# PV of three late head pairs with P as the weight in a decode kernel of two attention and MLP layers

## The chip, the cores and the metric

The kernel runs on one core of one Trainium2 chip. The metric is the time of one execution on the device, in microseconds; lower is better. Three executions of the kernel before took 303.86, 305.12 and 305.42 us, with a median of 305.12 us.

## The reference

Four sequences decode one token each. A layer is an attention block and a gated MLP, and two such layers run one after the other with the same weights and the same K and V caches:

```python
x = x + _A_ref(_layernorm(x), A_k_cache, A_v_cache, A_wq, A_wo)
x = x + _B_ref(_layernorm(x), B_w_gate, B_w_up, B_w_down)
```

In `_A_ref`, q = x @ wq gives 32 heads of 128; four query heads share one of 8 K/V heads (grouped queries); scores over 4096 keys are scaled, a softmax gives P, the output of a head is P @ V, and all heads go through `wo`. Everything is bf16 at the border; K and V of one sequence and head are 4096 x 128, 1 MB each. `_B_ref` is sigmoid(x @ w_gate) * (x @ w_up) @ w_down with 1792 hidden features.

## The kernel before, in words

The work on the caches is cut into **units**: one layer, one sequence, one K/V head. Two neighbouring heads make a **pair** g; there are 32 pairs, in the order of the list `ORDER`. K and V of a unit are one slot each of SBUF, 32 keys to a partition. There are 12 slots, and four more once wq is done with. `RET` says which units of the first layer stay in SBUF for the second; the last three pairs before the end, 28, 29 and 30, belong to layer 1, sequence 3, and have their K (and one V) kept, so that only V of 56, 58, 59, 60 and 61 and K and V of the last pair's units 62 and 63 are loaded for them. All loads are issued by SyncE in the order of `LOADS`, by `pump` (L522), which issues as many as there are free slots; it is called wherever a slot comes free.

The main loop (L1821) has one iteration k for each pair. It scores the pair sg = k and does PV of the pair vg = k - 1. Instructions of an engine run in program order. Each pair goes through these steps, with the lines at which they are recorded:

- `k_turn` (L1149, record L1164): VectorE transposes K in place, whole or in two halves.
- `scores` (L1166, record L1180): q as the weight, K as the moving operand, 256 columns a matmul, over four strips of 32 PSUM partitions. 16 matmuls a unit.
- `smax` (L1213), `spread_max` (L1236, record L1240), `softmax` (L1250; the exponential is L1265, on ScalarE): the row maximum on VectorE, spread over the rows by TensorE, then exp. The sums are split on GpSimd (L1279), and `sums` (L1283, record L1288) and `inverse` bring 1/sum to all partitions.
- `ptrans` (L1305, record L1310): TensorE transposes P into PSUM (`PT`). P is then copied to `pT` in 16 pieces of 32 partitions, `SHARE[g]` groups of four on VectorE (L1338), the others on ScalarE (L1344). With `SHARE[g]` 6 it is a single ScalarE copy (L1325), the exponential writes P in another order of keys, and V comes in four pieces of 2 KB a partition (`by_quarters`, L503), since the order of keys over partitions differs. Pair 29 is such a pair, and so is pair 31, whose V is loaded in single pieces of 256 KB by `v_parts` (L510).
- `pv` (L1349), once for each unit: V as the weight (128 x 128), P as the moving operand, 4 columns repeated up to `PV_WIDE[g]` columns. 32 matmuls a unit, recorded at L1414, or at L1364 where V comes in quarters. The result stands with a head's 128 features on the partitions.
- `normalise` (L1496, record L1505): VectorE multiplies by 1/sum into `oT`.
- `wo_mm` (L1515): a pair's part of wo. With `WO_ROW[g]` 0, 32 matmuls with wo as the weight (L1566). With 1 or 2, oT is the weight and wo moves over four strips (L1536), ScalarE copies the rows out (L1545) and two fp32 matmuls with the selector `sel_f` turn them into columns (L1549); with 2 this turn comes later, at the next `do_steps`. `wo_add` (L1587) adds to x.

`PV_WIDE[g] < 2` chooses another way in `pv`: P as the weight, V moving, two strips for each unit. No pair uses it in the kernel before; `o_turn` (L1474) belongs to it.

Where a step stands within the iteration is written out in tables. For the iterations that matter here: in iterations 29 and 30 PV of pairs 28 and 29 comes after the exponential of the iteration's own pair, both units one behind the other; in iteration 31 the first unit of pair 30 comes before the spread of the maximum of pair 31, the second after its exponential is issued. Wo of pair 28 is in iteration 30, of pair 29 in iteration 31 (its turn delayed), of pair 30 after the loop's last scores, in iteration 32. Then follow PV of pair 31 (`pv_last`, L1431, record L1441), its wo (L1775), the last MLP (L920, L2018) and the output.

Of the kernel before, what the change touches and what calls it, by code (L numbers as in the profile page):

```python
# [5 lines left out]
dt = mybir.dt  # L6
# [98 lines left out]
)  # L105
# [41 lines left out]
)  # L147
# [6 lines left out]
}  # L154


# [154 lines left out]
def bass_interleave_layers__gqa_block_cached__glu_gated_glu__decode_kernel(  # L311
# [73 lines left out]
    mask_f = sbt([P, 4, 2, 4, REP], dt.bfloat16, "mask_f")  # L385
    sel_f = sbt([P, 2, 2], dt.float32, "sel")
    SEL = 2 * REP * any(w < 2 for w in PV_WIDE)
    o_sel = sbt([P, 2, SEL], dt.float32, "o_sel") if SEL else None
    strip_b = sbt([P, 16], dt.bfloat16, "strip_b")
# [6 lines left out]
    xc_sb = sbt([P, KD, Bn], dt.float32, "xc")  # L396
    norm = sbt([P, KD + 10, Bn], dt.float32, "norm")
    sq_sb, newt = norm[:, 0:KD + 1, :], norm[:, KD + 1:, :]
    lnsum, blk_f, vpe, nt_a, nt_b, nt_c, nt_y, rs = [newt[:, i, :] for i in range(8)]
    y0i = newt[:, 8, :].bitcast(dt.int32)  # L400
    xc_bf = sbt([P, KD, Bn], dt.bfloat16, "xc_bf")
# [258 lines left out]
    def head_masks():  # L660
# [15 lines left out]
        for u in range(2):  # L676
# [29 lines left out]
        )  # L706
        id4 = ident_bf.rearrange("p (u e w) -> p u e w", u=2, e=2)
        dve(
            lambda e: e.tensor_tensor(sel_f[:, :, :], id4[:, :, 0, 0:2], id4[:, :, 1, 0:2], ALU.add),
            reads=IDENT,  # L710
            writes=["sel"],
        )
        if SEL:
            dve(
                lambda e: e.tensor_tensor(o_sel[:, :, :], id4[:, :, 0, 0:SEL], id4[:, :, 1, 0:SEL], ALU.add),
                reads=IDENT,
                writes=["o_sel"],
            )
        if SEL or any(WO_ROW):
# [585 lines left out]
    def ptrans(g):  # L1305
# [15 lines left out]
        if SHARE[g] > 5:  # L1321
            to = pT.rearrange("p x n j h -> p (x n j h)")
            keys = [f"pT_{x}{a}" for x in range(XJ) for a in ("", "_0", "_1", "_2")]
            if SHARE[g] == 6:
                act(lambda e: e.activation(to, PT[:, 0:2 * P], ACTF.Copy), reads=["PT"], writes=keys)  # L1325
            else:
                dve(lambda e: e.tensor_copy(to, PT[:, 0:2 * P]), reads=["PT"], writes=keys)
            return
        src = PT[:, 0:256].rearrange("p (n a h) -> p n a h", n=16, h=REP)
        for x in range(XJ):  # L1330
            for a in range(4):
                dst = pT[32 * a:32 * a + 32, x].rearrange("p n j h -> p j n h")
                frm = src[32 * x:32 * x + 32, :, a, :].rearrange("p (j n) h -> p j n h", j=2)
                key = f"pT_{x}"
                wr = [key if a == 3 else f"{key}_{a}"]
                if x in (1, 3)[:SHARE[g]]:
                    dve(
                        (lambda dst, frm: lambda e: e.tensor_copy(dst, frm))(dst, frm),  # L1338
                        reads=["PT"],
                        writes=wr,  # L1340
                    )
                else:
                    act(
                        (lambda dst, frm: lambda e: e.activation(dst, frm, ACTF.Copy))(dst, frm),  # L1344
                        reads=["PT"],
                        writes=wr,
                    )

    def pv(i):  # L1349
# [6 lines left out]
        if by_quarters(i):  # L1356
# [20 lines left out]
            if l == 1 or not kept("v", i):  # L1377
                free.append(where.pop(("v", b, u)))
            return
        if PV_WIDE[g] < 2:  # L1380
            many = 2 - PV_WIDE[g]
            for x in range(XJ):
                fns = []
                for m in range(4 // many):
                    at = 2 * ul + m % 2
                    fns.append(
                        (lambda x, m, at: lambda e: e.matmul(
                            O_ps[p][32 * at:32 * at + 8 * many, 0:2 * P * many],
                            lhsT=pT[:, x, 4 * ul + many * m:4 * ul + many * (m + 1), :, :].rearrange("p c j h -> p (c j h)"),
                            rhs=vv[:, x * JG + 2 * many * m:x * JG + 2 * many * (m + 1), :],  # L1390
                            start=(x == 0 and m < 2),
                            stop=(x == XJ - 1 and m >= 4 // many - 2),
                        ))(x, m, at)
                    )
                key = f"pT_{x}"
                rd = [f"s{s}", key] + [f"{key}_{a}" for a in range(3)]
                if ul == 0 and x == 0:
                    S.group("pe", fns, reads=rd, writes=[f"O{p}"])
                else:
                    S.last_write[f"O{p}"] = S.group("pe", fns, reads=rd)  # L1400
            done = l == 1 or not kept("v", i)
            if ul == 0:
                stage.clear()
            elif done and stage:
                free.append(stage.pop())
            if done:
                stage.append(where.pop(("v", b, u)))
            return
# [64 lines left out]

    def o_turn(g):  # L1474
        p = g % 2
        many = 2 - PV_WIDE[g]
        s = stage.pop()
        o_raw = slot[s].bitcast(dt.float32)[:, 0:2 * P * many]
        act(lambda e: e.activation(o_raw, O_ps[p][:, 0:2 * P * many], ACTF.Copy), reads=[f"O{p}"], writes=slot_keys(s))
        fns = []  # L1480
        for n in range(2 * many):
# [9 lines left out]
            )  # L1491
        S.group("pe", fns, reads=slot_keys(s) + ["o_sel"], writes=[f"O{p}"])
        free.append(s)
        pump()

    def normalise(g):  # L1496
        if PV_WIDE[g] < 2:
            o_turn(g)
        l, b, u = seq[2 * g]
# [321 lines left out]
    for k, (sg, vg) in enumerate(plan):  # L1821
# [34 lines left out]

        def pv_second():
            pv(2 * vg + 1)
            pump()

        def divide():
            normalise(vg)
            normed[seq[2 * vg]] = k
# [29 lines left out]
        if pv_first and both:  # L1893
            pv(2 * vg)
            pump()
            if pv_both:
                pv_second()
# [17 lines left out]
        if both and not pv_first and not pv_late:  # L1915
            pv(2 * vg)
            pump()
        wo_at(2)
        do_steps(k, 5)
        second_turn(1)  # L1920
        if pv_late:
            pv(2 * vg)
            pump()
        if sg == NP - 1 and LAST & 3 == 0:
# [39 lines left out]
        if sg is not None and sg != NP - 1:  # L1964
            ptrans(sg)
        wo_at(3)
        do_steps(k, 7)
        second_turn(2)
        if vg is not None and sg is not None and vg in ends:
            close(vg, k)  # L1970
        if k == NP - 3:
            wo_sums()
        if sg is not None and EARLY[sg]:
            sums(sg)
            inverse(sg)
            for ul in range(2):
                pv(2 * sg + ul)
                pump()
            normalise(sg)
            normed[seq[2 * sg]] = k  # L1980
            if sg in ends:
# [150 lines left out]
```

## Time and profile before

| What | Value |
|---|---|
| Median of three timed executions | 305.12 us |
| Span of the profiled execution, first to last instruction | 306.1 us |
| TensorE matmul busy | 224.3 us, 73% of the span, 4993 instructions |
| VectorE busy | 205.7 us, 67% |
| ScalarE busy | 131.2 us, 43% |
| GpSimd busy | 26.0 us, 9% |
| Moved from HBM | 116.66 MB, 381 GB/s over the span |
| Mean granted TensorE clock | 0.883 |
| Chain that ended last | DMA 45%, PE 30%, DVE 12%, SPq 5%, ACT 4%, issue 3% |

The span of 306.1 us is the profiled execution's own time; the timed executions are others. The chain is the work that ended last, followed back from the last instruction, each step to what released it. "Issue" in it is time in which an engine waited for nothing that the profile shows. PE is TensorE, PEld its weight loads, DVE VectorE, ACT ScalarE, POOL GpSimd, SP SyncE. An instruction is named by the line of the kernel that made it, its output and its inputs, with the shape as partitions x elements. All shares are means over the whole span; the stretch that the change touches is the last 30 us of it.

### The profile page before, as it was taken

How to read it: one execution, taken by the hardware profiler on the slowest of the kernel's cores; microseconds unless marked ns; L12 is line 12 of the kernel's file. 1: busy time of each engine (PE TensorE's matmuls, PEld its weight loads, DVE VectorE, ACT ScalarE, POOL GpSimd, SP SyncE). 2: the span in 40 equal slices, each digit the busy share in tenths (PEclk: the TensorE clock that was granted, in tenths of full speed). 3: DMA queues.
4: the chain of work that ended last, by engine and by line, in shares of the span. 5: the costliest groups of instructions: out<-in, count | busy, mean ns of one | idle time of the engine just before them, and what ended most of it. 6: DMA issues, size and time to landing. Idle time of an engine off the chain costs nothing.

```text
span 306.1 us, 11460 instructions
## 1 busy us (share of the span) xinstructions
PE 224.3 (73%) x4993; PEld 157.6 (51%) x4993; DVE 205.7 (67%) x600; ACT 131.2 (43%) x521; POOL 26.0 (9%) x107
## 2 busy tenths in 40 slices
PE   0384386864687888688886777888868688987886
PEld 0331043543464466566554554665546456556676
DVE  4755677885766368875854997566788668357743
ACT  1031243552205246564451874627772443646310
POOL 0000000000000010000001110001000000012200
PEclk9999999999579897979999857589788979599977
DMA  7999999999999979999999999999999999999900
GB/s 283 420 397 415 422 414 416 418 418 421 418 416 403 388 295 418 423 415 416 388 394 378 415 422 421 419 418 422 420 416 418 413 412 415 400 345 411 377 18 3
DMA packets 20094, 117.40 MB, mean 384 GB/s; under 512 B 1992, under 2 KB 1996, under 8 KB 7500
## 3 DMA queue, kind: packets, MB, share of 16 engines
q1 hardware_dynamic: 20044, 116.67, 93.9%
q8 instruction: 39, 0.64, 0.8%
q14 instruction: 11, 0.09, 0.1%
HBM read 116.66 MB, written 0.00 MB: 381 GB/s over the span
## 4 chain that ended last, share of the span: by engine, by line
DMA 45%; PE 30%; DVE 12%; SPq 5%; ACT 4%; issue 3%; POOL 0%; POOLq 0%; DVEq 0%; ACTq 0%
DMA slot<-in_A_v_cache_dram 22%; DMA slot<-in_A_k_cache_dram 12%; PE O_ps L1414 9%; DMA wd<-in_B_w_down_dram 6%; DVE slot L1164 6%; DMA wo<-in_A_wo_dram 5%; PE S_ps L1180 5%; ACT pT L1344 2%; SPq L550 2%; SPq L528 2%; PE M_ps L636 2%; PE O_ps L1566 2%; PE M_ps L1034 1%; PE M_ps L1087 1%; DVE wo L651 1%
## 5 line engine op out<-in xcount | busy, mean ns | idle before, releaser
L1164 DVE STREAM_TRANSPOSE slot<-slot 128x1024 f32<-128x1024 f32 (+1 forms) x61 | 100.9, 1663 | 7.0 <-DMA slot<-in_A_k_cache_dram 6.9
L1344 ACT ACTIVATE pT<-PT 32x64 bf16<-32x64 f32 x392 | 84.3, 215 | 31.9 <-PE PT L1310 26.9
L1414 PE MATMUL O_ps<-pT,slot 128*128 128x32 bf16 (+2 forms) x1888 | 65.8, 190 | 16.2 <-DMA slot<-in_A_v_cache_dram 9.6
L1414 PEld LDWEIGHTS O_ps<-pT,slot 128*128 128x128 bf16 x1888 | 59.6, 101 | 23.3 <-DMA slot<-in_A_v_cache_dram 10.6
L1180 PE MATMUL S_ps<-slot,qz 128*32 128x256 bf16 x1008 | 48.9, 329 | 12.5 <-DVE slot L1164 7.2
L1265 ACT ACTIVATE pe<-S_ps,small 128x256 bf16<-128x256 f32 x32 | 15.2, 474 | 63.3 <-DVE small L1253 63.2
L1180 PEld LDWEIGHTS S_ps<-slot,qz 128*32 128x32 bf16 x1008 | 25.3, 107 | 24.8 <-DVE slot L1164 9.2
L1279 POOL TENSOR_TENSOR small<-small 128x1 f32<-128x1 f32 x64 | 12.4, 193 | 217.6 <-ACT pe L1265 215.1
L646 ACT ACTIVATE wo<-M_ps 128x512 bf16<-128x512 f32 x14 | 8.3, 595 | 35.0 <-PE M_ps L636 35.0
L1338 DVE CAST pT<-PT 32x64 bf16<-32x64 f32 x88 | 19.4, 221 | 5.6 <-PE PT L1310 4.1
L1566 PE MATMUL O_ps<-oT,wo 128*128 128x32 bf16 x576 | 19.7, 188 | 1.1 <-issue 0.5
L636 PE MATMUL M_ps<-wo,row 64*128 64x512 bf16 x56 | 13.3, 565 | 9.1 <-DVE wo L651 5.5
L1566 PEld LDWEIGHTS O_ps<-oT,wo 128*128 128x128 bf16 x576 | 18.2, 101 | 2.1 <-DVE oT L1505 1.1
L1217 DVE TENSOR_REDUCE small<-S_ps 128x1 f32<-128x256 f32 x32 | 13.2, 413 | 8.0 <-PE S_ps L1180 7.8
L903 POOL TENSOR_TENSOR qz<-qc,norm 128x128 bf16<-128x128 bf16 x32 | 12.6, 399 | 45.5 <-ACT qc L889 45.5
L1240 PE MATMUL MS<-row_max,mask_f 128*128 128x16 bf16 x64 | 6.6, 176 | 13.1 <-DVE row_max L1223 12.6
L651 DVE CAST wo<-M_ps 128x512 bf16<-128x512 f32 x14 | 9.5, 680 | 9.6 <-PE M_ps L636 9.5
L1505 DVE TENSOR_TENSOR oT<-O_ps,rden 128x8 bf16<-128x8 f32 x31 | 4.9, 159 | 14.4 <-PE O_ps L1414 9.8
L1240 PEld LDWEIGHTS MS<-row_max,mask_f 128*128 128x128 bf16 x64 | 4.3, 107 | 19.2 <-DVE row_max L1223 17.7
L1199 PE MATMUL MS<-ident_bf 128*128 128x256 bf16 x69 | 12.2, 316 | 0.4
L1310 PE MATMUL PT<-ident_bf,pe 128*128 128x128 bf16 x64 | 10.0, 245 | 2.9 <-ACT pe L1265 2.6
L1253 DVE CUSTOM_DVE_ANT_0 row_max<-MS,small 128x16 bf16<-128x16 f32 x32 | 7.0, 217 | 7.3 <-PE MS L1240 7.1
(143 smaller groups left out, 231.1 us busy)
## 6 DMA issues: line engine op xcount, KB each, us to landing
slot<-in_A_v_cache_dram SPq DMA_DIRECT2D x49, 1024.0 KB, 12.5
slot<-in_A_k_cache_dram SPq DMA_DIRECT2D x43, 1024.0 KB, 11.3
wq<-in_A_wq_dram SPq DMA_DIRECT2D x4, 1024.0 KB, 7.8
wo<-in_A_wo_dram SPq DMA_DIRECT2D x8, 512.0 KB, 15.8
wq<-in_A_v_cache_dram SPq DMA_DIRECT2D x3, 1024.0 KB, 12.3
slot<-in_A_v_cache_dram SPq DMA_DIRECT2D x8, 256.0 KB, 13.6
wg<-in_B_w_gate_dram SPq DMA_DIRECT2D x2, 896.0 KB, 18.9
wu<-in_B_w_up_dram SPq DMA_DIRECT2D x2, 896.0 KB, 16.2
```

What stands on the lines that cost most here:

```text
L636: (lambda h, i, rows: lambda e: e.matmul(ps[h][:, :], lhsT=spread_w[i][rows, :], rhs=wo_sb[rows, c + i, :], start=(i == 0), stop=(i == 1), ...
L651: lambda e: e.tensor_copy(wo_sb[:, c + 1, :], ps[1][:, :]),
L903: lambda e: e.tensor_tensor(qz_sb[z][:, :, 0:4 * REP].rearrange("p i (a r) -> p i a r", r=REP), qc_sb[:, b, u:u + 2, :, :].rearrange("p u ...
L1164: dve(lambda e: e.transpose(kf, kf), writes=[f"s{st}"])
L1180: (lambda t, b2, e_, w0, s: lambda e: e.matmul(S_ps[p][32 * s:32 * s + 8 * REP, 0:2 * P], lhsT=qzf[:, w0:w0 + 8 * REP], rhs=ktv[:, :, s, : ...
L1217: lambda e: e.tensor_reduce(m, S_ps[p][:, 0:2 * P], AX.X, ALU.max),
L1265: lambda e: e.activation(to, frm, ACTF.Exp, bias=nm_sb[p], scale=exp_scale, accum_out=sm_sb[p][0],),
L1279: (lambda n: lambda e: e.tensor_tensor(sm_sb[p][n + 1], sm_sb[p][n], top(sm_sb[p][n]), ALU.subtract))(n),
L1338: (lambda dst, frm: lambda e: e.tensor_copy(dst, frm))(dst, frm),
L1344: (lambda dst, frm: lambda e: e.activation(dst, frm, ACTF.Copy))(dst, frm),
L1414: (lambda x, c, j: lambda e: e.matmul(O_ps[p][:, ul * OW:ul * OW + PV_WIDE[g]].rearrange("p (w n) -> p w n", n=REP), lhsT=vv[:, x * JG + c ...
L1566: (lambda c, r: lambda e: e.matmul(wide_out(O_ps[p], OWO + c, nb), lhsT=wo_sb[:, u * REP + r, bass.ds(2 * P * (c // 2) + c % 2, P, step=2) ...
```

## The change

PV of pairs 28, 29 and 30 is done with P as the weight: `PV_WIDE` is 1 for them. A new function `pv_rows` takes both units of a pair together: 32 matmuls, each with 8 columns of P as the weight and 256 columns of V (two keys to a partition) moving, over four strips of PSUM partitions, two for each unit. The result stands as rows. `o_copy` copies them from PSUM to the pair's second V slot on ScalarE, and `o_turn` makes columns of them with two fp32 matmuls against `o_sel`, and then calls `normalise`. `TURN[k]` says where in the iteration that is: behind P's transpose (1; for pairs 28 and 29) or directly where the division stood (0; for pair 30, in iteration 31). `SHARE[30]` becomes 6: P of pair 30 is copied at once on ScalarE, and its V is loaded in pieces of 2 KB. The selectors `sel_f` and `o_sel` become one tile, and the layer norm's scratch loses one of its rows (`nt_y` shares that of `nt_b`).

```diff
-    1, 0, 0, 2, 1, 6, 2,
+    1, 0, 0, 2, 1, 6, 6,
...
-    32, 32, 64, 48, 64, 48, 64, 48,
+    32, 32, 64, 48, 1, 1, 1, 48,
...
+TURN = (
+    1, 1, 1, 1, 1, 1, 1, 1,
+    1, 1, 1, 1, 1, 1, 1, 1,
+    1, 1, 1, 1, 1, 1, 1, 1,
+    1, 1, 1, 1, 1, 1, 1, 0,
+    1,
+)
...
+    sel_f = o_sel[:, :, 0:2]
...
+            if PV_WIDE[g] < 2:
+                to = to.rearrange("p (m j h) -> p j m h", j=2, h=REP)
+                frm = frm.rearrange("p (j m h) -> p j m h", j=2, h=REP)
...
+    def pv_rows(g):
...
+        for x in range(4):
+            fns = []
+            for m in range(4 // many):
+                for ul in range(2):
+                    at = 2 * ul + m % 2
+                    fns.append(
+                        (lambda x, m, ul, at: lambda e: e.matmul(
+                            O_ps[p][32 * at:32 * at + 8 * many, 0:2 * P * many],
+                            lhsT=pT[:, x, 4 // many * ul + m, :],
+                            rhs=vv[ul][:, x, m, :],
+                            start=(x == 0 and m < 2),
+                            stop=(x == 3 and m >= 4 // many - 2),
+                        ))(x, m, ul, at)
+                    )
+            rd = [f"s{s}" for s in units] + (keys if pieces else [f"pT_{x}"] + [f"pT_{x}_{a}" for a in range(3)])
...
+        for ul in range(2):
+            assert l == 1 or not kept("v", 2 * g + ul)
+            stage.append(where.pop(("v", b, u + ul)))
+        free.append(stage.pop(0))
...
-    def o_turn(g):
+    def o_copy(g, k):
+        p = g % 2
+        s = stage.pop()
+        o_raw = slot[s].bitcast(dt.float32)[:, 0:2 * P * (2 - PV_WIDE[g])]
+        act(
+            lambda e: e.activation(o_raw, O_ps[p][:, 0:2 * P * (2 - PV_WIDE[g])], ACTF.Copy),
+            reads=[f"O{p}"],
+            writes=slot_keys(s),
+        )
+        turning.append((g, s, o_raw, k))
+
+    def o_turn():
...
+        normalise(g)
+        normed[seq[2 * g]] = k
...
+        def pv_start():
+            if PV_WIDE[vg] < 2:
+                o_turn()
+                pv_rows(vg)
+                o_copy(vg, k)
+            else:
+                pv(2 * vg)
+            pump()
...
         def divide():
+            if PV_WIDE[vg] < 2:
+                if TURN[k] == 0:
+                    o_turn()
+                return
...
         if sg is not None and sg != NP - 1:
             ptrans(sg)
+        if TURN[k] == 1:
+            o_turn()
```

More of the change, by code (lines that the diff above doesn't have):

```diff
@@ L385, in bass_interleave_layers__gqa_block_cached__glu_gated_glu__decode_kernel @@
     mask_f = sbt([P, 4, 2, 4, REP], dt.bfloat16, "mask_f")
-    sel_f = sbt([P, 2, 2], dt.float32, "sel")
-    SEL = 2 * REP * any(w < 2 for w in PV_WIDE)
-    o_sel = sbt([P, 2, SEL], dt.float32, "o_sel") if SEL else None
+    SEL = 2 * REP * (2 - min(PV_WIDE)) if min(PV_WIDE) < 2 else 0
+    o_sel = sbt([P, 2, max(SEL, 2)], dt.float32, "o_sel")
+    sel_f = o_sel[:, :, 0:2]
     strip_b = sbt([P, 16], dt.bfloat16, "strip_b")
@@ L1378, in pv @@
                 free.append(where.pop(("v", b, u)))
[L1379 to L1407, printed above, removed]
             return
@@ L1968, in bass_interleave_layers__gqa_block_cached__glu_gated_glu__decode_kernel @@
         second_turn(2)
+        if TURN[k] == 2 or vg in ends:
+            o_turn()
         if vg is not None and sg is not None and vg in ends:
@@ L1975, in bass_interleave_layers__gqa_block_cached__glu_gated_glu__decode_kernel @@
             inverse(sg)
-            for ul in range(2):
-                pv(2 * sg + ul)
+            if PV_WIDE[sg] < 2:
+                o_turn()
+                pv_rows(sg)
+                o_copy(sg, k)
                 pump()
-            normalise(sg)
-            normed[seq[2 * sg]] = k
+                o_turn()
+            else:
+                for ul in range(2):
+                    pv(2 * sg + ul)
+                    pump()
+                normalise(sg)
+                normed[seq[2 * sg]] = k
             if sg in ends:
```

65 lines of the change are left out of this document (39 added, 26 removed).

## The prediction

> **What bounds the kernel now.** I read the page first, then the chain of waits from 277 us on, then the timeline and the busy times by stretch there.
>
> ```profile
> span 306.1 us, 11460 instructions
> ...
> q8 instruction: 39, 0.64, 0.8%
> ```
>
> All terms below are of this one execution, 306.1 us from first to last instruction; the three timed runs have a median of 305.12 us, 1.0 less. I work out a difference in the execution and take it off the median. The second row is the instruction fetch: 39 packets, 0.64 MB, so 16.4 KB each.
>
> ```profile
> 277.66 1.98 PE O_ps L1414 x64
> ...
> 279.97 0.46 issue
> ...
> 282.33 0.39 ACT row L1545
> ...
> 282.77 0.64 PE O_ps L1549 x4
> ...
> 284.04 1.51 PE O_ps L1364 x56
> 285.55 1.17 issue
> ...
> 288.13 0.54 PE O_ps L1536 x16
> 288.67 0.84 PE O_ps L1414 x24
> ...
> 289.93 0.45 PE O_ps L1549 x4
> ...
> 290.40 0.22 PE MS L1240 x2
> ...
> 292.17 0.22 PE MS L1288 x3
> ...
> 292.56 0.54 issue
> 293.10 0.99 PE O_ps L1566 x27
> 294.09 1.28 PE O_ps L1441 x32
> ```
>
> This is the chain of waits (start, length, what). The reader should see that no transfer stands in it: from 277 us on the end is set by TensorE's program order. PV of pairs 28, 29 and 30 are the pieces at 277.66, 284.04 and 288.67 (the second unit of pair 30 follows later, off the chain), and pair 31's PV begins at 294.09. Three pieces are "issue": TensorE stood still and waited for nothing that the profile shows, 0.46, 1.17 and 0.54 us. In the program's order 127 matmuls, each with its weight load, lie between one of these stops and the next: some 256 instructions, which at 16.4 KB a packet is 64 bytes each. So I read the stops as the ends of fetched blocks, reached before the next block was there. They belong to a place in the instruction count, not to the instruction where they stand.
>
> **The change part by part.** *PV in strips.* Pair 28 and pair 30 drop 64 full-array matmuls of 64 columns, pair 29 drops 64 of 48; each gets 32 of 256 columns, 8 weights wide, over four strips. The same shape over four strips is there already, the scores of pair 29:
>
> ```profile
> 275.35 1.14 PE L1180 MATMUL S_ps<-slot,qz 128*32 128x256 bf16 x32
> ...
> 278.22 0.47 ACT L1265 ACTIVATE pe<-S_ps,small 128x256 bf16<-128x256 f32 x1
> ```
>
> So 32 take 1.14 us to the last result, and the next instruction can follow after some 0.89 (0.25 of it is the last one's way through the array). That is 1.14 against 1.98 for pair 28. *Rows turned.* Each pair adds a ScalarE copy out of PSUM (0.39, the row of L1545, same 128x256 shape) and two fp32 matmuls (four records, 0.64, the row of L1549; 8 moving columns instead of 4, which I price the same; its bounds are 0.64 and, at the column rate of the scores, 0.1 more). With 0.1 and 0.05 for the hand-overs (282.77 stands 0.05 behind the copy's end) the result of a pair comes 1.2 us after its PV. That wait is new: behind the turn on TensorE stand the next scores, behind the copy on ScalarE the next pair's P copy.
>
> Going from strips to the full array is charged at nothing: the full matmuls of 288.67 follow those in strips of 288.13 (0.54 long) without a gap. If a switch cost something, the bound is one matmul's way, 0.25 (a rival below).
>
> *Pair 28.* PV 277.55 to 278.75. The exponential of pair 29 ends at 278.69, so its P transpose fits in the shadow of the copy (278.85 to 279.24); turn 279.3 to 279.95; scores of pair 30 start at 279.8, about where they start now (two of them run before the stop at 279.97). PV's 0.8 us is eaten by copy and turn. But the program has 28 matmuls fewer before the block's end (32 less, 4 added), so the 0.46 stop moves from the 2nd to the 30th of these scores, reached at 280.65, after the time at which the block came (280.43): 0.46 us goes. What is late next is VectorE:
>
> ```profile
> 279.82 2.30 DVE L1164 STREAM_TRANSPOSE slot<-slot 128x2048 f32<-128x2048 f32 x1
> ...
> 287.57 1.89 DVE L1338 CAST pT<-PT 32x64 bf16<-32x64 f32 x8 [0.22 <-issue]
> 289.49 0.42 DVE L1217 TENSOR_REDUCE small<-S_ps 128x1 f32<-128x256 f32 x1
> ```
>
> Pair 28's division stands in front of the K transpose on VectorE and now ends at 280.1, so the 2.30 us runs to 282.4 instead of 282.1, and the maximum of pair 30 behind it is 0.25 later. Of the gain 0.1 to 0.3 is left at the spread of the maximum (283.15).
>
> *Pair 29.* Scores of pair 31 (first unit) 283.25, PV 283.7 to 284.85: no block end lies in it any more, so it ends 2.2 us before today's 287.1 (8 of the 64 follow the stop's end at 286.72). The copy waits behind the exponential of pair 30 on ScalarE (to 285.3), so: copy to 285.65, turn to 286.3, second scores of pair 31 at 286.4, Wo rows of pair 29 at 287.05 instead of 288.13. Some 1.0 is left.
>
> *P of pair 30 in one copy.* The 8 casts on VectorE (1.89 us) and 8 copies on ScalarE become one ScalarE copy like that of pair 29. The maximum of pair 31, at 289.49 behind the casts, moves to about 287.2. *V of pair 30 in 2 KB pieces.* PV of pair 30 now needs both units at its start:
>
> ```profile
> L550 SPq DMA_DIRECT2D slot<-in_A_v_cache_dram x1: 2867/2867/2867, 271.5 to 271.5; - x1
> ...
> DMA to landing us min/median/max: 15.8/15.8/15.8
> ```
>
> This is the second unit's transfer: issued 271.5, landed 287.3. Every load takes a slot that is free before pair 28's PV, so none starts at another time, and the pump behind a turn finds nothing left to issue on SP; POOL's order is untouched. The rate:
>
> ```profile
> 282.66:286.07 3.41, 2.78 (x78) 2.42 (x79) 2.82 (x7) 0.62 (x3) 0.43 (x3) 1.00 1.00 404
> 286.07:289.48 3.41, 2.76 (x71) 2.12 (x70) 2.00 (x10) 2.10 (x9) 1.53 (x5) 1.00 1.04 387
> 289.48:292.90 3.42, 2.70 (x57) 2.28 (x57) 2.32 (x12) 1.06 (x4) 0.39 (x2) 1.00 0.43 153
> 292.90:296.31 3.41, 3.21 (x90) 3.21 (x90) 1.43 (x10) 0.00 (x0) 0.00 (x0) 0.50 0.02 5
> ```
>
> (stretch, length, busy of PE, PEld, DVE, ACT, POOL, granted clock, DMA share, GB/s.) The first stretch moves mostly 8 KB pieces, 404 GB/s, the second mostly 2 KB pieces, 387: for 2.1 MB 0.2 us more; bounds 0 and 0.5. So V is there at 287.5. The last pieces, pair 31's, land 0.2 later too; DMA is all but idle after 292.9 (share 0.02) and their matmuls come after 293.
>
> *Pair 30.* Wo rows of pair 29 end at 287.4; PV waits for V until 287.5, its last issue is at 288.4, the turn of Wo's rows takes 0.45, and the spread of pair 31's maximum stands at 288.85 instead of 290.40: **1.55 us** earlier. Copy and turn of pair 30 lie beside pair 31's softmax (290.40 to 292.17 now, 1.77 long): they would end 1.3 us into it, so cost nothing; without that cover they cost 1.2. Behind it the stop of 0.54 at 292.56 has moved away: **0.54** more. The selector and the scratch of the layer norm change in the set-up, beside the first loads, and cost nothing; they are outside this stretch.
>
> *What comes back.* Two block ends lie in the rest: about the 9th matmul of pair 30's PV, and some 127 later, in Wo of the last pair's first unit. Each can cost 0 to 1.17 (the longest row). I take the middle row, 0.54, for both, as TensorE runs as dense there as at 292.56: **1.08 back**. Sum: 1.55 + 0.54 - 1.08 = **1.0 us** off. 306.1 becomes 305.1, and the median 305.12 becomes **304.1**.
>
> **The rivals.** *No stop remains on the path.* Strips give fewer instructions in the same time (32 pairs in 0.89 us against 56 in 1.51: the same pace, but 28 fewer a pair), and pair 30's wait for V lets the fetch catch up. Then 2.1 us are off: 303.0. Against it: the last 120 matmuls before the second block end follow without a wait.
>
> *The gain is eaten.* Both stops are long (1.17 each): 2.1 - 2.34, so 305.4. The same comes if the array has to run empty at each change between strips and full: some six new changes of 0.25, 1.5 in all, so 305.6. Against that speaks the pair of rows at 288.13 and 288.67, for it nothing here. The Trainium skill ("TensorEngine Tiling (Array Packing)", Key Properties) says that a change of tiling mode drains the array; by that rule this is what happens, and the trace, with no gap at 288.67, does not bear it out.
>
> *Slower: the clock is halved.* Granted clock changes at steps of 3.41 us. Weighing each matmul by its columns, a strip one by a quarter, the stretch at 282.66 holds some 3760 and the one at 286.07 some 4280, and the clock stays at 1.00; the one at 289.48 holds some 3050 and the next is at 0.50, though TensorE was busy for 2.70 of 3.42 us. PV in strips weighs 32 x 64 = 2048 where it weighed 4096 (pairs 28 and 30) or 3072. By my times 279.24 to 282.66 would hold 2048 (scores) + 1024 (Wo) + about 150 = 3220, 6% over the stretch that lost the clock. Should one of these fall below, scores and PV of 282.66 to 289.5 run at half pace: 0.43 + 0.86 for pair 29 and 0.43 + 0.37 + 0.86 for pair 30, of which 0.3 hides behind VectorE: 2.7 against the gain of 1.0, so 1.7 slower, 306.8. It decides from a count of about 3050 on, and the steps lie elsewhere in each run. The Trainium skill ("TensorE: Matmul & The Clock Gate", Part 1) halves the clock only after an idle window of about 3.4 us; by that no stretch here would lose it. The trace does not agree: 289.48 to 292.90 was 79% busy and lost it.
>
> **How the numbers follow.** Forecast 304.1 (303.2 to 305.0), chance 0.43; no stop 303.0 (302.4 to 303.8), 0.30; gain eaten 305.4, 0.14; half clock 306.8, 0.13. A measurement of this kernel tells about 0.5% from no change, 1.5 us: faster is below 303.6, slower above 306.65. Faster: 0.24 of the second case and 0.07 of the first, 0.31. Slower: 0.11 of the last and 0.02 of the third, 0.13. The rest, 0.56, lies within. The range 302.6 to 306.2 leaves out most of the half-clock case and the low end of the second.
>
> **What would show it.** Right: 32 PV matmuls in about 1.14 us each pair, no stop inside PV of pair 29, the maximum of pair 31 directly behind its scores near 287.2, PV of pair 30 ended by its V transfer, pair 31's PV near 293. Wrong: PV in strips over 1.5 us (strips not overlapping), a clock of 0.50 between 282 and 289, a stop over 1.2 us, or V of pair 30 landing after 288.

## The result, and the profile after

Thirteen executions of the changed kernel have a median of 305.63 us (303.68 to 307.50), thirteen of the kernel before 303.95 us (301.50 to 305.57). The ratio is 1.0061, with a 95% interval of 1.0035 to 1.0086: **slower by 0.6%, 1.9 us** (1.7 between the medians), where 1.0 us less was forecast. The ratios of the experiments below leave out executions that lie more than 1.5% above the shortest of their kernel, which are six of twelve in after_light (those over 304.1 us), so that its median over all twelve is given beside its ratio.

The traced execution of the kernel after has a span of 303.6 us. From its chain of waits, from 283 us on (start, length, what):

```profile
283.19 0.57 PE O_ps L1568 x16
...
284.17 1.24 issue
285.41 1.88 PE O_ps L1379 x24
287.28 0.96 PE O_ps L1581 x4
...
290.09 1.00 PE O_ps L1598 x32
291.09 1.28 PE O_ps L1460 x32
```

Against the chain before: the stops in PV of pair 29 (1.17) and in wo of pair 30 (0.54) are gone; wo of pair 30 is one piece of 32. A new idle piece of 1.24 us stands in front of PV of pair 30 (TensorE itself stands idle for 1.68, from 283.73), and that PV takes 1.88 us and not the 0.89 of the forecast. The chain calls the idle piece "issue". What ends it, by its time, is a transfer, V of unit 61 (the experiment v60_twice tests this); its issue and its way to landing:

```profile
L560 SPq DMA_DIRECT2D slot<-in_A_v_cache_dram x1: 4455/4455/4455, 268.6 to 268.6; - x1
...
DMA to landing us min/median/max: 16.8/16.8/16.8
```

Issued at 268.56, it lands at 285.32, and PV starts at 285.41. What waits behind it is seen on VectorE and in the spread on TensorE (timeline; in brackets the idle time before the instruction and what ended it):

```profile
283.07 0.42 DVE L1222 TENSOR_REDUCE small<-S_ps 128x1 f32<-128x256 f32 x1 [0.58 <-PE S_ps L1185]
...
283.73 0.19 DVE L1228 TENSOR_TENSOR row_max<-strip_b,small 128x32 f32<-128x32 bf16 x1
288.27 0.16 DVE L1619 TENSOR_TENSOR xT<-xT,O_ps 128x8 f32<-128x8 f32 x1 [4.35 <-PE O_ps L1581]
```

```profile
288.09 0.20 PE L1245 MATMUL MS<-row_max,mask_f 128*128 128x16 bf16 x2
```

The maximum of pair 31 is ready at 283.92, directly behind its scores, as forecast. TensorE spreads it only at 288.09, because PV of pair 30 and the turn of wo's rows stand in front of the spread in its program. The three PVs of the changed kernel one by one (stretch, length, TensorE busy and weight loads of L1379 alone, granted clock, DMA share, GB/s):

```profile
273.00:276.00 3.00, 1.05 (x32) 0.60 (x32) 1.00 1.04 391
279.00:282.00 3.00, 1.05 (x32) 0.73 (x32) 1.00 1.05 387
285.00:288.00 3.00, 1.88 (x32) 0.98 (x32) 0.50 0.90 330
```

The third runs at half clock, granted from 284.4 to 294.6.

**The kernel before, traced a second time.** The trace on which the prediction rests spans 306.1 us. The changed kernel's traced execution of 305.39 us has a span of 303.6, 1.8 less than its time; with as much around it the first trace of before is one of 307.9 us, above all thirteen timed ones (of the 122 executions of the kernel before that were timed beside the experiments, four took as long). A second trace of the unchanged kernel (before_again, span 300.8 us) shows another layout. Its chain:

```profile
264.27 16.00 DMA wq<-in_A_v_cache_dram
...
280.32 0.77 PE O_ps L1364 x24
...
283.96 0.85 PE O_ps L1414 x24
...
285.73 0.22 PE MS L1240 x2
...
287.89 0.48 issue
...
289.35 0.80 PE O_ps L1441 x32
```

Here the chain comes from a transfer: the second unit's PV of pair 29 starts when V of unit 59 has landed. V of unit 61 is issued at 268.5 and lands at 285.3, as in the changed kernel, and the spread of pair 31's maximum follows 0.45 us behind it, without waiting for it (only the second unit's PV, behind the spread, needs it). In the first trace the same spread stood 3.1 us behind that landing (290.40 against 287.30). Its clock was 0.50 from 258.8 to 269.0, and TensorE came late to everything behind.

So the two traces compare like this: spread of pair 31's maximum 285.73 before and 288.09 after, 2.36 later; PV of pair 31 289.35 and 291.09, 1.74 later (the stop of 0.48 is gone); from there to the end 11.4 and 12.5 us, as the clock is at half up to 294.6 in the changed kernel and at full up to 295.8 in the kernel before.

### The profile page after: what moved, and what is told of

Its sections match the earlier page's. It is cut to its first block, busy times and chain, and to the rows that moved or that the text cites. A ratio compares the mean times of both kernels' runs of the same rounds, so it can differ in the third digit from the quotient of the medians.

```text
span 303.6 us, 11281 instructions
## 1 busy us (share of the span) xinstructions
PE 219.2 (72%) x4909; PEld 154.9 (51%) x4909; DVE 203.7 (67%) x592; ACT 130.4 (43%) x517; POOL 26.0 (9%) x107
## 4 chain that ended last, share of the span: by engine, by line
DMA 39%; PE 27%; DVE 19%; ACT 6%; SPq 5%; issue 3%; POOL 0%; POOLq 0%; DVEq 0%
DMA slot<-in_A_v_cache_dram 15%; DMA slot<-in_A_k_cache_dram 13%; DVE slot L1169 10%; PE O_ps L1433 7%; DMA wd<-in_B_w_down_dram 6%; DMA wo<-in_A_wo_dram 5%; PE S_ps L1185 4%; ACT pT L1353 3%; SPq L560 2%; PE O_ps L1598 2%; SPq L538 2%; PE M_ps L646 1%; PE M_ps L1039 1%; DVE small L1222 1%; ACT pe L1270 1%
## 5 line engine op out<-in xcount | busy, mean ns | idle before, releaser
L1353 ACT ACTIVATE pT<-PT 32x64 bf16<-32x64 f32 x384 | 82.3, 214 | 29.5 <-PE PT L1315 24.6
L1433 PE MATMUL O_ps<-pT,slot 128*128 128x32 bf16 (+2 forms) x1792 | 62.6, 190 | 14.4 <-DMA slot<-in_A_v_cache_dram 7.3
L1433 PEld LDWEIGHTS O_ps<-pT,slot 128*128 128x128 bf16 x1792 | 56.8, 101 | 20.9 <-DMA slot<-in_A_v_cache_dram 9.0
L1185 PE MATMUL S_ps<-slot,qz 128*32 128x256 bf16 x1008 | 46.3, 317 | 14.0 <-DVE slot L1169 9.0
L1185 PEld LDWEIGHTS S_ps<-slot,qz 128*32 128x32 bf16 x1008 | 24.5, 104 | 25.6 <-DVE slot L1169 10.9
L1284 POOL TENSOR_TENSOR small<-small 128x1 f32<-128x1 f32 x64 | 12.4, 193 | 219.2 <-ACT pe L1270 216.7
L1347 DVE CAST pT<-PT 32x64 bf16<-32x64 f32 x80 | 17.7, 221 | 4.3 <-PE PT L1315 3.1
L1537 DVE TENSOR_TENSOR oT<-O_ps,rden 128x8 bf16<-128x8 f32 x31 | 5.0, 160 | 13.9 <-PE O_ps L1433 10.6
## 6 DMA issues: line engine op xcount, KB each, us to landing
slot<-in_A_v_cache_dram SPq DMA_DIRECT2D x49, 1024.0 KB, 12.5
wo<-in_A_wo_dram SPq DMA_DIRECT2D x8, 512.0 KB, 15.5
wq<-in_A_v_cache_dram SPq DMA_DIRECT2D x3, 1024.0 KB, 13.6
```

The source lines that it names most:

```text
L1185: (lambda t, b2, e_, w0, s: lambda e: e.matmul(S_ps[p][32 * s:32 * s + 8 * REP, 0:2 * P], lhsT=qzf[:, w0:w0 + 8 * REP], rhs=ktv[:, :, s, : ...
L1284: (lambda n: lambda e: e.tensor_tensor(sm_sb[p][n + 1], sm_sb[p][n], top(sm_sb[p][n]), ALU.subtract))(n),
L1433: (lambda x, c, j: lambda e: e.matmul(O_ps[p][:, ul * OW:ul * OW + PV_WIDE[g]].rearrange("p (w n) -> p w n", n=REP), lhsT=vv[:, x * JG + c ...
```

## The experiments

Four theories. **W**: PV of pair 30 needs V of both its units at its start, and it stands in front of the spread of pair 31's maximum; in the kernel before only the second unit's PV, behind that spread, needs the later transfer. **C**: PV in strips keeps less of the array busy, and TensorE loses its clock. **T**: copy and turn cost each pair what its shorter PV gives. **D**, formed after the first eight results: in most executions the late V loads pace the last pairs, so TensorE's shorter order has nothing to gain. Each ratio below is to the kernel before, timed beside it.

**before_again**: the kernel before, unchanged.

> The kernel before, once more, for a second trace and to see how far two timings of one kernel differ. All theories: ratio 1.000, within 0.004. Theory W (PV of pair 30 now waits for both V units in front of the spread of pair 31's maximum) says that here the first unit's V has landed when its PV begins (no wait there), and the second unit's V lands within 2 us of that, during or before pair 31's softmax. Theory C (the lighter PV in strips loses the clock) says that granted clock is 1.00 in the 3.41 us stretches from pair 29's PV to pair 30's PV.

0.9986 (0.9958 to 1.0013), as it must be; its trace is the one above, and what W and C expected of it came: V of unit 60 landed (282.76) before its PV, V of unit 61 within 2 us of that PV's start, and the clock is 1.00.

**p30_old**: only pairs 28 and 29 in strips.

```diff
-    1, 0, 0, 2, 1, 6, 6,
+    1, 0, 0, 2, 1, 6, 2,
...
-    32, 32, 64, 48, 1, 1, 1, 48,
+    32, 32, 64, 48, 1, 1, 64, 48,
```

> Pair 30 as before (V as the weight, V in 8 KB pieces, P copied in 16 pieces), pairs 28 and 29 in strips. Theory W: the loss goes, 1.5 us less than the changed kernel, ratio to before 0.997 to 1.001. Theory C: two of the three light PVs stay, so most of the loss stays, 1.003 to 1.005. Theory T (each pair's copy and turn cost 0.3 to 0.5 us on the path): two thirds of the loss stay, 1.004.

0.9988 (0.9957 to 1.0019). The loss is gone with pair 30, and pairs 28 and 29 neither gain nor lose. That is against T (1.004), and against C as expected here (1.003 to 1.005).

**p30_only**: only pair 30 in strips.

```diff
-    32, 32, 64, 48, 1, 1, 1, 48,
+    32, 32, 64, 48, 64, 48, 1, 48,
```

> Pair 30 as in the change (strips, 2 KB pieces, one copy), pairs 28 and 29 as before. Theory W: the whole loss is here, ratio to before 1.005 to 1.009. Theory C: one light PV of three, the stretch before PV of pair 30 keeps its weight, 1.001 to 1.003. Theory T: a third of the loss, 1.002.

1.0054 (1.0014 to 1.0094): with p30_old, the loss is pair 30's. By itself the interval still holds what C (1.001 to 1.003) and T (1.002) expected. The stop in PV of pair 29 is back, as its place in the instruction count has it (after 56 of 64 matmuls, as before), and PV of pair 30 at full clock takes 0.87 us (chain):

```profile
284.41 1.16 issue
...
287.51 0.87 PE O_ps L1379 x32
```

In this execution V of unit 61 landed at 286.39, before TensorE came to PV of pair 30, so this one trace does not show the wait; its clock was at half from 257.1 to 267.4, and TensorE was late as in the first trace of the kernel before.

**v60_twice**: PV of pair 30 reads the first unit's V for both units, so that nothing waits for unit 61. V of unit 61 does not enter the result, and the rows are kept in the first unit's slot.

```diff
         units = [where["v", b, u + ul] for ul in range(2)]
+        if g == NP - 2:
+            units = units[:1] * 2
...
-        free.append(stage.pop(0))
+        free.append(stage.pop(1 if g == NP - 2 else 0))
```

> The changed kernel, but PV of pair 30 reads the first unit's V for both units (its rows are kept in that V's slot); this changes what pair 30 adds to the output. All work and all transfers stay, only the wait for the second unit's V goes. Theory W (that wait stands in front of the spread of pair 31's maximum and costs 1.5 us): 1.0 to 1.7 us less than the changed kernel, ratio to before 0.998 to 1.003. Theory C (the lighter PV loses the clock): no gain by that, 1.005 to 1.006.

0.9993 (0.9962 to 1.0024). The instructions are those of the changed kernel; only the wait is away (PV of pair 30 starts at 285.15, V of unit 61 lands at 285.88), and the interval does not touch that of the changed kernel (1.0035 to 1.0086). So the loss needs this wait: W is shown, and with it that the 2 KB pieces and the single copy, which are both in here, do not make the loss. That nothing is gained beside it fits its chain: PV of pair 29 starts at the landing of V of unit 59, and a stretch at half clock (282.8 to 286.2) makes PV of pair 30 1.46 long:

```profile
265.11 15.39 DMA wq<-in_A_v_cache_dram
...
280.63 1.07 PE O_ps L1381 x32
...
285.15 1.46 PE O_ps L1381 x31
```

**pv30_behind**: PV of pair 30 behind the exponential of pair 31.

```diff
-    71, 124, 3, 38, 71, 44, 6, 4,
+    71, 124, 3, 38, 71, 44, 6, 1,
```

> The changed kernel with PV of pair 30 put behind the exponential of pair 31 is issued, instead of in front of the spread of its maximum; nothing else. Theory W: the spread of the maximum no longer stands behind V's landing, so pair 31's softmax (1.8 us) lies beside the wait, and 1.0 to 1.5 us come back: ratio to before 1.001 to 1.003. Theory C: the work and its weight stay, 1.006. Theory T: 1.006.

1.0024 (0.9986 to 1.0062): W expected 1.001 to 1.003, C and T 1.006, and the interval reaches both. The spread no longer waits (it stands in front of PV), but copy and turn of pair 30 lose their cover (chain):

```profile
285.80 1.08 PE O_ps L1379 x32
...
287.33 0.63 PE O_ps L1516 x4
...
290.73 0.42 PE S_ps L1807 x8
291.15 0.58 issue
```

PV, copy and turn stand on the chain one behind the other, and the stop that the prediction put into wo of the last pair's first unit is there, 0.58 us after 8 of its 16 matmuls.

**rows_by_unit**: the same function, first unit where PV stood, second unit behind the exponential, two strips at a time.

```diff
-    def pv_rows(g):
+    def pv_rows(g, uls=(0, 1)):
...
-                for ul in range(2):
+                for ul in uls:
...
-                pv_rows(vg)
-                o_copy(vg, k)
+                pv_rows(vg, (0,) if vg == NP - 2 else (0, 1))
+                if vg != NP - 2:
+                    o_copy(vg, k)
...
+            elif vg == NP - 2:
+                pv_rows(vg, (1,))
+                o_copy(vg, k)
```

> The changed kernel with PV of pair 30 in rows unit by unit: 16 matmuls of the first unit over two strips where all 32 stood, 16 of the second over the other two strips behind the exponential of pair 31, as the two units stood in the kernel before. Two strips at a time make the matmuls slower, about 0.8 us a unit. Theory W: the spread of pair 31's maximum no longer waits for the second unit's V, 1.0 to 1.5 us come back, ratio to before 1.000 to 1.003. Theory C: the weight in the stretches stays, 1.005 to 1.007.

1.0035 (0.9998 to 1.0072), inconclusive between W (1.000 to 1.003) and C (1.005 to 1.007). Its chain:

```profile
285.21 0.87 PE O_ps L1379 x16
...
286.70 0.99 PE O_ps L1379 x16
...
287.71 0.39 ACT slot L1502
...
288.14 0.63 PE O_ps L1518 x4
```

16 matmuls in two strips take 0.87 and 0.99 us, as long as 32 in four, so this PV costs twice, and copy and turn stand behind it on the chain as in pv30_behind.

**p30_onecopy**: pair 30 keeps V as the weight, unit by unit, but its P is copied at once and its V comes in 2 KB pieces.

```diff
-    32, 32, 64, 48, 1, 1, 1, 48,
+    32, 32, 64, 48, 1, 1, 64, 48,
```

> Pairs 28 and 29 in strips; pair 30 with V as the weight, unit by unit as before, but with P in one ScalarE copy and V in 2 KB pieces as in the change. Theory W: no wait of both units, so no loss; and the maximum of pair 31 no longer stands behind 8 casts on VectorE, 0.3 to 0.8 us faster than with 16 copies: ratio to before 0.996 to 0.999. If the 2 KB pieces were the loss (0.3 us a MB at the end): 1.002 to 1.006.

1.0019 (0.9980 to 1.0058). The gain that W expected (0.996 to 0.999) and the loss by the pieces (1.002 to 1.006) both reach into the interval, so this run does not decide; on the pieces v60_twice does. Its chain tells what binds when TensorE is early:

```profile
267.41 17.67 DMA slot<-in_A_v_cache_dram
...
285.12 1.11 PE O_ps L1412 x32
```

V of unit 61 lands at 285.08 and the second unit's PV starts at 285.12. From this landing to the end of the span it takes 15.0 us here, 15.5 in before_again and 18.3 in the changed kernel.

**fill31**: 8 more matmuls of 256 columns, on unused PSUM, in front of wo's rows in iteration 31, where TensorE waits for V.

```diff
-    (18, 7): 3, (22, 2): 4, (25, 5): 2, (33, 1): 1,
+    (18, 7): 3, (22, 2): 4, (25, 5): 2, (31, 1): 8, (33, 1): 1,
```

> The changed kernel with 8 idle matmuls (128x256, results not used) on TensorE in front of pair 29's Wo rows in iteration 31, where TensorE waits for V of pair 30 afterwards anyway (1.2 us or more in the trace after). They weigh 2048 columns in the stretch that lost the clock. Theory C: clock 1.00 when PV of pair 30 runs, its 32 matmuls take 1.1 us instead of 1.9, and 0.8 to 1.3 us come back: ratio to before 1.002 to 1.003. Theory W alone: no change, 1.006; if TensorE doesn't wait there, 0.4 to 0.9 us slower, 1.008.

1.0038 (1.0004 to 1.0071), between what C (1.002 to 1.003) and W (1.006) expected, and no clear difference from the changed kernel. In its trace (span 300.9 us, among its shortest executions) the clock holds, and PV of pair 30 and the turn of wo's rows have their full-clock lengths:

```profile
285.29 0.87 PE O_ps L1379 x32
286.16 0.57 PE O_ps L1581 x4
```

V of unit 61 landed at 284.61 here, before TensorE came to it, so that this trace does not show the wait.

**before_light, after_light, p30_old_light**: V of units 56, 58, 59, 60 and 61 loaded by half in the kernel before, in the changed one and in p30_old. The other half of a slot keeps what stood there.

```diff
+            if kind == "v" and n >= 56:
+                if by_quarters(n):
+                    dst, src = dst[:, 0:2, :], src[:, 0:2, :]
+                else:
+                    w = NJ * DH // 2
+                    dst, src = dst[:, 0:w], src[:, 0:w]
             S.dma(
```

> The kernel before with V of units 56, 58, 59, 60 and 61 loaded by half (the other half of the slot keeps what stood there, so the output is not the reference's); no instruction of the engines is changed. 2.6 MB less, at 2.5 to 2.7 us per MB up to 6.5 us earlier for the last of them. Theory D (in usual executions the late V loads pace the last pairs: in before_again PV of pair 29 waits for V of unit 59, and the last V lands 10.4 us before the end): with the loads out of the way the order of TensorE sets the end, about 2 us earlier: ratio to the kernel before 0.990 to 0.995. Rival E (TensorE's order binds already, as my prediction had it): the ratio is 0.997 to 1.000, and the loads' landing earlier gives nothing.

> The changed kernel with the same five loads halved (the other half of each slot keeps what stood there). Theory D: the wait of pair 30's PV for both units goes, and what is left is what the prediction counted, 1.0 to 2.1 us: 0.993 to 0.997 of before_light, so 0.983 to 0.992 of the kernel before; TensorE is the last releaser of pair 30's PV. Rival C (lighter PV loses the clock, or copies and turns cost what PV gives): the change still loses or gives nothing, 1.000 to 1.008 of before_light, with a granted clock of 0.50 under PV of pair 30.

> p30_old (pair 30 as before, pairs 28 and 29 in strips) with the same five loads halved (the other half of each slot keeps what stood there). Theory D: pairs 28 and 29 give here what the loads hid in p30_old: the stop in PV of pair 29 and the shorter PV, 0.5 to 1.5 us, 0.995 to 0.998 of before_light. Rival E: nothing, as with the full loads (0.9988, interval 0.9957 to 1.0019). If after_light gains and this does not, the gain is pair 30's; if this gains and after_light does not, pair 30 in strips costs by itself, without any wait for V.

before_light 0.9958 (0.9922 to 0.9993), after_light 0.9919 (0.9869 to 0.9969), p30_old_light 0.9930 (0.9891 to 0.9970). Unchanged instructions are faster with earlier loads, so loads pace the end in part: 0.9958 lies between D (0.990 to 0.995) and E (0.997 to 1.000). The three intervals overlap; and the medians over all executions are 302.85, 304.15 and 302.40 us, after_light's twelve executions lying anywhere between 299.6 and 308.3. p30_old_light is 0.9930 / 0.9958 = 0.997 of before_light, what D had for it, but not apart from 1. The ratios say that the loss goes. The medians do not: after_light's is 1.3 us above before_light's, p30_old_light's is not. By the expectation for p30_old_light that would mean that pair 30 in strips costs something without any wait for V; the times leave it open. The traces say more. Chain of before_light:

```profile
280.91 1.18 issue
...
285.79 0.22 PE MS L1246 x2
...
288.79 0.80 PE O_ps L1447 x32
```

and of after_light:

```profile
281.81 0.58 PE S_ps L1191 x15
282.40 0.16 PE MS L1299 x3
282.56 0.54 PE O_ps L1574 x16
283.10 0.87 PE O_ps L1385 x32
283.97 0.57 PE O_ps L1587 x4
...
287.39 0.82 PE O_ps L1466 x32
```

With V out of the way PV of pair 30 follows wo's rows without a gap, the spread of pair 31's maximum stands at 284.39 instead of 285.79, 1.40 us earlier (forecast: 1.55), and PV of pair 31 1.40 earlier. But from there to the end after_light takes 12.4 us and before_light 10.6, and after_light has a clock of 0.50 from 288.0 on.

**after_light_2, after_light_fill, after_fill4**: a second trace of after_light, and 6 more matmuls between the spread of pair 31's maximum and wo of pair 30, where TensorE stands idle, in after_light and in the changed kernel.

```diff
-    (18, 7): 3, (22, 2): 4, (25, 5): 2, (33, 1): 1,
+    (18, 7): 3, (22, 2): 4, (25, 5): 2, (31, 4): 6, (33, 1): 1,
```

> after_light once more (five V loads by half, the other half of the slots keeps what stood there), for a second trace: its 12 executions lie between 299.6 and 308.3, the traced one was among the shortest, 301.6. Theory C: a longer execution shows a clock of 0.50 in more of the stretches between 258 and 300 than the first trace. Rival: the same clock, and longer waits for transfers.

> after_light (five V loads by half, the other half of the slots keeps what stood there) with 6 more matmuls of 256 columns on unused PSUM between the spread of pair 31's maximum and the wo of pair 30, where TensorE stands idle for 1.6 us in after_light (284.6 to 286.2). They weigh 1536 columns, so the stretch that held 2856 and lost the clock would hold some 4400. Theory C (what is left of the loss is the clock: lighter PV brings a stretch of 3.41 us under some 3000 weighted columns): the clock stays at 1.00 through 292, the tail from pair 31's PV to the end takes 10.8 to 11.5 us instead of 12.6, and the median falls from 304.15 to 300.5 to 302. Theory not C: the median stays at 303.5 to 305, or rises by what the 6 cost.

> The changed kernel with the same 6 matmuls in the same place. Theory W alone (the wait for V of unit 61): the wait stands in front of them, so nothing changes, 1.004 to 1.008 of the kernel before. Theory W with C: the stretch before PV of pair 30 (2390 columns) still loses the clock, only its return comes earlier: 1.002 to 1.006.

after_light_2 took 303.94 us. Theory C expected more time at half clock between 258 and 300 than in the first trace, and that did not come: 13.6 us here (258.7 to 265.5, 289.4 to 292.8, 296.2 to 299.6), 15.4 there. The first of these lies ahead of the change and makes everything behind it late: the spread of pair 31's maximum is at 286.75, 0.96 later than in before_light. Counted from the spread of pair 29's maximum it comes after 11.23 us, in after_light after 12.25 and in before_light after 13.55 (285.79 less 272.24). after_light_fill has 0.9913 (0.9880 to 0.9945), nearly the ratio of after_light (0.9919); its median over all seven executions is 301.71 us, where after_light had 304.15. The busy times by clock stretch (length, then busy of PE, PEld, DVE, ACT, POOL, granted clock) in after_light and in after_light_fill:

```profile
284.60:288.00 3.40, 2.58 (x72) 2.35 (x73) 2.34 (x15) 1.05 (x4) 0.39 (x2) 1.00 0.00 0
288.00:291.40 3.40, 3.40 (x98) 3.40 (x93) 0.72 (x7) 0.00 (x0) 0.00 (x0) 0.50 0.02 5
```

```profile
287.00:290.40 3.40, 3.31 (x93) 3.08 (x91) 2.26 (x15) 0.51 (x3) 0.39 (x2) 1.00 0.00 0
290.40:293.80 3.40, 2.92 (x89) 2.84 (x90) 1.09 (x8) 0.15 (x1) 0.00 (x0) 1.00 0.02 5
```

Six matmuls more, and the stretch behind them keeps the clock; the median falls to where theory C had it. The two medians were timed apart and spread widely, and the ratios hardly differ, so the traces support C and the times do not prove it. In the changed kernel itself the six matmuls bring 1.0037 (0.9999 to 1.0076), which neither theory can claim: the wait for V stands in front of them. Its trace shows that wait alone, as the clock is 1.00 from 256.5 to 300.9 (timeline):

```profile
285.63 0.27 PE L1379 MATMUL O_ps<-wq,pT 128*8 128x256 bf16 x1 [1.13 <-ACT row L1577]
...
287.11 0.19 PE L1245 MATMUL MS<-row_max,mask_f 128*128 128x16 bf16 x2
```

V of unit 61 landed at 285.54; the spread stands 1.57 us behind it, where it was 0.45 in before_again.

**onecopy_fill**: p30_onecopy with the same six matmuls.

> p30_onecopy (pair 30 by units with V as the weight, but P in one copy and V in 2 KB pieces; pairs 28 and 29 in strips) with the same 6 matmuls. If the clock of the last 12 us is what keeps it from a gain, 0.992 to 0.997 of the kernel before; if the last V transfer is, as its trace has it (PV of pair 31 waits 0.77 us for its last piece), 0.998 to 1.004.

1.0001 (0.9964 to 1.0037): no gain, as the expectation had it for the transfer (0.998 to 1.004) and not for the clock (0.992 to 0.997). It names the wrong transfer: the pause in p30_onecopy's PV of pair 31 comes after 28 of 32 matmuls, and a V piece serves 8, so it is no wait for a piece but looks like a block end. V of unit 61 starts p30_onecopy's chain; in onecopy_fill's trace it landed at 285.83, and the second unit's PV stood behind the six matmuls until 287.25, so that they cost there what they may have saved. Why p30_onecopy gains nothing stays open. None of the versions is faster than the kernel before by more than its interval, unless loads are halved.

## Why the prediction was wrong

**The step that failed** is "PV waits for V until 287.5" and the 1.55 us behind it. The wait was seen; it was mis-sized. It was counted from one trace in which TensorE was 3 us late against the transfers (half clock from 258.8 to 269.0), so that V of unit 61 seemed to come just as TensorE was ready for it. Where TensorE is not late, as in before_again, after and after_fill4, V comes later than TensorE: 16.8 us from issue to landing in both kernels, in a queue that moves 384 GB/s with a DMA share of 1.04 (row below). In before_again the old order had used that: its spread stands 0.45 us behind the landing. The new order puts 0.87 us of PV and 0.57 of turn between landing and spread, 0.1 + 0.87 + 0.57 = 1.54 where 0.45 was: 1.1 later at full clock, as after_fill4 has it (1.57 behind the landing). At the half clock of the traced execution they take 1.88 and 0.96, 1.4 more; together 2.5, and measured between the traces 2.36. The prediction's own times have a slip beside it: wo's rows at 287.05 and 0.54 long end at 287.59, not at 287.4, which takes some 0.1 off the 1.55.

**Right in kind, hidden in size.** PV in strips took 1.05 us (1.14 forecast), copy and turn about 1.2 (0.38 and 0.61, and the hand-overs), pair 29 had no stop, pair 31's maximum moved directly behind its scores, and behind pair 28's division VectorE's K transpose was next (chain of after):

```profile
276.20 0.17 DVE oT L1537
276.37 2.22 DVE slot L1169
```

With the loads halved the spread stood 1.40 earlier in one trace of after_light; that this is so near to 1.55 is in part luck, as the same stretch came out 1.30 and 2.32 shorter in its two traces, counted from the spread of pair 29's maximum. In p30_old the part of pairs 28 and 29 was worth 0.9988 (0.9957 to 1.0019), nothing that can be told. In v60_twice and before_again PV of pair 29 waits for V of unit 59, so that time gained before it is given back there. In p30_old's own trace that V landed at 279.71, ahead of its PV at 280.12, and the chain runs through VectorE's K transposes and casts up to 284.27, not through TensorE. The chain of the first trace held no transfer in the stretch, and the prediction took that for the kernel's and not for that execution's.

**The 2 KB pieces** cost nothing that shows: 16.8 us to landing before and after, and v60_twice, which has them, is at 0.9993 (0.9962 to 1.0024).

**The stops that come back** were charged 1.08. The one in wo of the last pair showed in pv30_behind, 0.58 (0.54 forecast), and in the changed kernel none did, behind a wait and at half clock.

**The rivals.** *No stop on the path* was true of the traced execution, and gave nothing, because V was late. *The gain is eaten* by a drain of 0.25 us at each change between strips and full array: after_light speaks against it. By its timeline the full-array matmuls of the sums begin at 282.33 (the last score in strips ends at 282.40), wo's rows in strips at 282.49 (282.56), and the full-array turn at 283.90 (283.97, the end of PV in strips): no group waits until the one before has ended. *The clock is halved*, given 0.13, happened in the traced execution, by the count that the rival named: matmuls weighed by columns and share of the array make 2390 in the stretch from 281.0 to 284.4, and the next is at 0.50. The wait for V had a part in emptying that stretch (0.67 of the 0.87 us that TensorE stood idle in it), so W and C are not independent here. The Trainium skill ("TensorE: Matmul & The Clock Gate", Part 1) gives an idle window of about 3.4 us as the condition; the trace does not agree, as TensorE was busy for 2.53 us of those 3.40:

```profile
281.00:284.40 3.40, 2.53 (x50) 1.62 (x43) 1.84 (x5) 1.32 (x5) 1.96 (x7) 1.00 1.04 384
```

The slower side of the forecast was built on the clock above all; the rival that decided, both units' V at once, stood in it as a step of the likeliest case, at a cost of 0.1 us.

The clock also goes without that wait. PV of pair 30 in strips takes both units' work ahead of the spread and leaves less behind it, during pair 31's softmax. In p30_only, after_light and after_light_2, where V had landed in time, and in after and v60_twice, the clock is at 0.50 during PV of pair 31 or right behind it, and from the start of that PV to the end it takes 12.4 or 12.5 us; in before_again, p30_old and fill31, which keep the clock there, 11.3 to 11.7. (The first trace of the kernel before lost it too, 12.0.) That this is not the whole loss v60_twice shows, which has this long end and is not slower.

**Open** stays how the 1.9 us divide between wait and clock: fill31 (1.0038) and after_fill4 (1.0037) lie below 1.0061, but their intervals overlap with it.

## What to carry to other kernels

When two steps are merged into one, the merged step waits for the later of their inputs, and it stands where the earlier one stood: ask what is queued behind it there. A landing time read from one trace is worth little if that execution's compute was late; set the transfer's own clock (issue to landing) against a second trace before a wait is priced at nothing. Work taken off an engine that the transfers pace comes back as idle time, and on TensorE the idle time can cost the clock of the next stretches, as from 284.4 on here.

## What the runs showed of the hardware

In these traces the granted clock changes at steps of 3.41 us, and busy time alone does not tell when; columns weighed by the share of the array tell it better. In before_again TensorE was busy for 2.13 us of a stretch (a weighted count of 3280) and kept the clock, and for 3.04 us of a later one (3060) and lost it at 295.8; 2.58 of 3.40 us lost it in after_light (2856). The rows of before_again:

```profile
278.80:282.20 3.40, 2.13 (x75) 1.73 (x64) 2.36 (x5) 0.57 (x2) 1.37 (x5) 1.00 1.01 401
```

```profile
292.40:295.84 3.44, 3.04 (x114) 2.95 (x111) 2.23 (x13) 0.59 (x2) 0.00 (x0) 1.00 0.02 5
```

The bound of about 3050 in the prediction is not sharp: counts of 2888 (v60_twice, at 276.0) and 2584 (rows_by_unit, at 287.1) kept the clock too. Some matmul records may be missing from a trace, so this is no law.

A PV of 16 matmuls over two strips took as long as one of 32 over four (0.87 us in rows_by_unit and in fill31): strips left empty saved no time here.
